# Attention and a two-layer network: tiles projected in another order, key sums behind the denominator, another order of DMAs

## The chip, the cores and the metric

The kernel runs on one core of a Trainium2 chip. The time is that of the device, in microseconds (us), as the median of several executions. An execution that is profiled beside those gives the trace; all rows below are of such an execution. Engines: PE is TensorE's matmul and PEld its weight load, DVE is VectorE, ACT is ScalarE, POOL is GpSimd, SP is SyncE, which here issues nearly all DMAs in the order of one queue.

## What is computed

Two parts follow each other. The first is linear attention over 8 batches of 8 heads with 576 rows of 64 elements: queries and keys are projected to 128 features, the largest absolute value of a row is taken off, and both exp(x) and exp(-x) are features. The second is a two-layer network over the 4608 rows of the result, with a function in between that is close to a cube for small values.

```python
def phi(x):
    proj = np.einsum('bhsd,df->bhsf', x, w_phi)
    proj = proj - np.max(np.abs(proj), axis=-1, keepdims=True)
    return np.concatenate([np.exp(proj), np.exp(-proj)], axis=-1)
q_p, k_p = (phi(q), phi(k))
kv = np.einsum('bhsf,bhsd->bhfd', k_p, v)
z = np.sum(k_p, axis=2)
num = np.einsum('bhsf,bhfd->bhsd', q_p, kv)
den = np.einsum('bhsf,bhf->bhs', q_p, z)[..., None] + 1e-06
x = (num / den)        # heads side by side: 4608 x 512
h = x @ w_in           # 512 x 2048
out = (h - np.tanh(h)) @ w_out
```

Weights of the second part come as 64-bit floats and are taken apart into 32-bit ones with integer operations on the core.

## The kernel before

**Units and periods.** The attention runs over 32 units (`units`, NU = 32), each a batch with a pair of heads. `period(i)`, for i from 0 to 32, does a step of several units at once: `a` is unit i (projection), `c` is unit i-1 (its key-value product and the transposes of its queries), `p` is unit i-2 (numerator, key sums, denominator), `r` is unit i-3 (reciprocal of the denominator), `r2` is unit i-4 (division and store of the result to `xs`). Each engine does its instructions in the order in which `period` writes them (`tc.manual_schedule`). No scheduler moves them.

**Projection.** A unit's queries and keys lie behind each other in `qk`, 1152 columns, which are 9 tiles of 128 (j = 0 to 8). Tiles 0 to 3 are queries, the first half of tile 4 is the last 64 query rows, its second half the first 64 key rows, and tiles 5 to 8 are keys. `project(u, r)` does a round r of them (`ROUNDS`, L202) into the PSUM tile `pp`, of which there is one (`ps_pj`, one buffer); DVE takes the maximum (`m`, L224), `less_max` subtracts it into `t` (L231) and so frees `pp` for the next round. A period has rounds 0, 1 and 2 with 2, 3 and 4 tiles: 8, 12 and 16 PE instructions in the trace, since each 32-bit product is two.

**Keys.** `k_exp` (ACT, L260) makes the key features `kp`: half of tile 4 from round 1, in the unit's own period; tiles 5 to 8 from round 2, one period later. `kv` (PE, L266, tile `pc`) multiplies them with `v`; `kv_copy` brings the product out. POOL adds the five key tiles: `kadd` does three additions in the period of `c`, into the tile `t` of round 2, `kadd_last` the fourth a period later. `ksum` (PE, L285, tile `pk`) adds over the partitions with four products with ones, between `kv` and round 2. `turn` transposes `kvt` and `kst` (tiles `ptk`), and `denom` (PE, L333, tile `pd`) needs its copy `kv..s` (ACT, L311).

**Queries.** `q_side` transposes them on PE (`ptr` L247, `ptt` L241) and makes `qe` on ACT (L251, L255). `num` (L318, tile `po`) uses them in the next period.

**The denominator.** `denom_copy` (ACT, L348, `dd`), a DMA that spreads it over partitions (`dn`, L353), the reciprocal on DVE (`rn`, L361), a DMA to DRAM (`rr`, L362), two DMAs that read it back as broadcasts (`rb`, L369), the product on DVE (`den_mul`, L374) and the store (`x_store`, L377).

**Weights.** One of 32 pieces of 512 KB is loaded in each period (`dec_load`, tile `raw`), and taken apart by `dec_0` (ACT, L168), `dec_1` (DVE, L172 and L173) and `dec_2`, `dec_3` (DVE, L176, L180). `split_w` then makes a high and a low part. `behind(x)` is a POOL copy of one column (`mark`, L187) which keeps POOL's later instructions behind whatever writes x.

**SP's order in a period:** dn, qk of the next unit, the store, rr, both rb, the weight piece, v of the next unit. Each waits in this queue for what it needs: rb for rr's landing, the store for `den_mul`.

The second phase (from L515) runs 12 groups of 384 rows over 16 slices of the hidden layer, and reads `xs` and the split weights.

Of the kernel before, what the change touches and what calls it, by code (L numbers as in the profile page):

```python
# [32 lines left out]
def tile_linear_attention_moe(  # L33
# [88 lines left out]
    with ExitStack() as c1:  # L122
# [79 lines left out]
        ROUNDS = ((0, 2), (2, 5), (5, 9))  # L202

        def project(u, r, where=None):
            j0, j1 = ROUNDS[r]
# [5 lines left out]
            for j in range(j0, j1):  # L211
                for e in range(2):
                    hs = slice(e * D, (e + 1) * D)
                    nc.tensor.matmul(  # L214
                        heads[e][:, (j - j0) * F : (j - j0 + 1) * F], u.qk[hs, j * P : (j + 1) * P], wph[hs, :], start=True, stop=True
                    )
# [40 lines left out]
        def k_exp(u, r):  # L257
            rows, x, j0, j1 = (slice(SR, P), u.t[1][SR:P, :, 2:3, :], 0, 1) if r == 1 else (slice(0, P), u.t[2], 1, 5)
            for s in range(2):
                nc.scalar.activation(u.kp[rows, :, j0:j1, s, :], x, AF.Exp, scale=1.0 - 2.0 * s)  # L260
# [9 lines left out]
        def kadd(u):  # L270
            x = u.t[2].rearrange("p e a f -> p (e a f)")[:, 0 : 4 * F].rearrange("p (e s f) -> p e s f", e=2, s=2)
            nc.gpsimd.tensor_tensor(x, u.kp[:, :, 1], u.kp[:, :, 2], ALU.add)
            nc.gpsimd.tensor_tensor(x, x, u.kp[:, :, 3], ALU.add)
            nc.gpsimd.tensor_tensor(x, x, u.kp[:, :, 4], ALU.add)
            u.ss = [x]

        def kadd_last(u):
            nc.gpsimd.tensor_tensor(u.ss[0], u.ss[0], u.kp[:, :, 0], ALU.add)

        def ksum(u):  # L280
            u.pk = ps_d.tile([P, 512], F32, tag="po", name=f"pk{u.i}")
            parts = u.ss or [u.kp[:, :, j] for j in range(5)]
            for a, x in enumerate(parts):
                for n in range(4):
                    nc.tensor.matmul(  # L285
                        u.pk[n * 32 : (n + 1) * 32, 0:F], ones, x[:, n // 2, n % 2, :], start=(a == 0), stop=(a == len(parts) - 1)
                    )
# [124 lines left out]
        def period(i):  # L412
# [26 lines left out]
            if 0 <= n < 4 * AHEAD:
                if n % 2 == 0:  # L440
                    lows.extend(split_w(n // 2))
                lows.pop(0)()
# [12 lines left out]
            if a:  # L455
                less_max(a, 1)
            if r:
                den_recip(r)
                den_spread(r)
            if w:  # L460
                dec_2(w)
                dec_3(w)
                if i < NU:
                    dec.append(dec_load(i))
                behind(w.d[w.f])
            if c:
                if not last:
# [205 lines left out]
```

## Time and profile before

| what | us |
|---|---|
| median of 3 runs (1160.58 to 1161.43) | 1161.35 |
| the profiled execution, its own time | 1161.82 |
| its span | 1160.00 |
| start to the first regular period (period 2) | 20.83 |
| periods 2 to 30 (20.83 to 320.80) | 299.97 |
| periods 31 and 32 (320.80 to 345.0) | 24.2 |
| second phase (from 345.0) | 815.0 |

A row of the timeline gives the start in us from the span's start, the duration, engine, line, operation, the tile written and the tiles read, and the shape; "x8" are eight instructions merged; in brackets stands how long the engine was idle before, and what ended that. A row of groups gives busy us and the mean ns of one behind the bar. A row of windows gives the stretch, its length, the busy time and instructions of PE, PEld, DVE, ACT and POOL, the granted TensorE clock, the share of the DMA engines' time and GB/s. A row of waits gives the sum, the times and the longest. A row of DMA issues ends with the median us from issue to landing.

### The profile page before, as it was taken

What the parts mean: (1) busy time and instruction counts of PE and PEld (TensorE: products, weight loads), DVE (VectorE), ACT (ScalarE), POOL (GpSimd) and SP (SyncE); (2) the same over time, 40 slices, a digit from 0 to 9 for tenths busy, and PEclk for the clock granted to TensorE, in tenths of its full rate; (3) what the DMA queues carried; (4) which work ended last, traced back from release to release, by engine and by line L of the source; (5) the groups of instructions that cost most, each with busy time, mean ns of one, the idle gap of its engine ahead of it and who ended that gap; (6) DMA issues with size and microseconds to landing.
All of it is one profiled execution on the core that took longest, in us unless ns stands there. A gap on an engine that the chain in (4) does not pass through costs nothing.

```text
span 1160.0 us, 20769 instructions
## 1 busy us (share of the span) xinstructions
PE 1139.1 (98%) x7610; PEld 947.5 (82%) x7610; DVE 862.9 (74%) x1429; ACT 818.2 (71%) x1780; POOL 428.0 (37%) x437
## 2 busy tenths in 40 slices
PE   8999999999999999999999999999999999999997
PEld 6666666666658889999999999999999999999996
DVE  6888888888868777776777777677777767777665
ACT  4777777787778767776766766676777667676664
POOL 2666666666537632222222222222222222222222
PEclk9999999999999999999999999999999999999999
DMA  4565666665742010000100010010100001000000
GB/s 155 186 197 177 207 205 211 193 197 195 224 130 66 14 35 14 34 21 8 41 15 34 14 35 21 8 42 14 35 21 35 14 8 41 14 29 1 28 1 28
DMA packets 51175, 85.60 MB, mean 74 GB/s; under 512 B 13312, under 2 KB 28032, under 8 KB 51072
## 3 DMA queue, kind: packets, MB, share of 16 engines
q1 hardware_dynamic: 50912, 84.20, 22.7%
q8 instruction: 60, 0.98, 0.4%
q14 instruction: 43, 0.35, 0.1%
q10 hardware_dynamic: 160, 0.07, 0.0%
HBM read 65.08 MB, written 19.02 MB: 72 GB/s over the span
## 4 chain that ended last, share of the span: by engine, by line
PE 84%; DMA 8%; ACT 3%; DVE 2%; SPq 1%; issue 1%; POOL 1%; DVEq 0%; POOLq 0%; ACTq 0%
PE ph L535 34%; PE po L573 11%; PE po L571 11%; PE po L570 11%; PE pp L214 4%; PE pc L266 4%; PE po L318 3%; DMA dn<-dd 3%; DMA rr<-rn 3%; PE pd L333 2%; DMA rb<-rr 2%; PE ptt L241 2%; PE pk L285 1%; SPq L369 1%; DMA qk<-in_qkT 1%
## 5 line engine op out<-in xcount | busy, mean ns | idle before, releaser
L564 POOL TENSOR_TENSOR gl<-s,gh 128x384 fp32r<-128x384 f32 x192 | 196.3, 1022 | 568.0 <-ACT gh L563 566.5
L542 ACT ACTIVATE y<-ph 128x384 f32<-128x384 f32 x192 | 94.5, 492 | 237.8 <-PE ph L535 237.6
L535 PE MATMUL ph<-xh,wli 128*128 128x384 f32 x768 | 259.1, 337 | 0.8 <-POOL wli L97 0.8
L535 PE MATMUL ph<-xh,whi 128*128 128x384 f32 x768 | 258.6, 337 | 0.0
L535 PE MATMUL ph<-xl,whi 128*128 128x384 f32 x768 | 257.9, 336 | 0.0
L551 DVE SCALAR_TENSOR_TENSOR s<-s,y 128x384 f32<-128x384 f32 x192 | 110.1, 573 | 180.6 <-ACT s L544 180.4
L570 PE MATMUL po<-who,gh 128*128 128x512 f32 x576 | 227.1, 394 | 1.7 <-ACT gh L563 1.7
L571 PE MATMUL po<-wlo,gh 128*128 128x512 f32 x576 | 226.8, 394 | 0.0
L573 PE MATMUL po<-who,gl 128*128 128x512 f32 x576 | 164.4, 393 | 0.9 <-POOL gl L564 0.9
L535 PEld LDWEIGHTS ph<-xh,whi 128*128 128x128 f32 x768 | 144.3, 188 | 8.9 <-issue 0.5
L535 PEld LDWEIGHTS ph<-xl,whi 128*128 128x128 f32 x768 | 144.2, 188 | 8.3
L535 PEld LDWEIGHTS ph<-xh,wli 128*128 128x128 f32 x768 | 144.1, 188 | 1.2 <-POOL wli L97 1.2
L260 ACT ACTIVATE kp<-t 128x1024 f32<-128x1024 f32 (+1 forms) x128 | 88.5, 751 | 79.8 <-DVE t L231 73.2
L557 DVE COPY_PREDICATED s<-mk,th 128x384 f32<-128x384 uint32 x176 | 123.8, 703 | 18.5 <-DVE th L556 0.5
L573 PEld LDWEIGHTS po<-who,gl 128*128 128x128 f32 x576 | 107.9, 188 | 27.3 <-POOL gl L564 2.5
L570 PEld LDWEIGHTS po<-who,gh 128*128 128x128 f32 x576 | 107.9, 187 | 20.6 <-ACT gh L563 3.6
L224 DVE TENSOR_REDUCE m<-pp 128x4 f32<-128x512 f32 (+3 forms) x98 | 92.0, 940 | 42.5 <-PE pp L214 41.1
L571 PEld LDWEIGHTS po<-wlo,gh 128*128 128x128 f32 x576 | 108.2, 188 | 16.3
L544 ACT ACTIVATE s<-y,bias_t 128x384 f32<-128x384 f32 x192 | 118.3, 616 | 3.0 <-POOL gl L564 3.0
L550 ACT ACTIVATE mk<-y,bias_t 128x384 f32<-128x384 f32 x192 | 117.7, 613 | 0.5 <-DVE s L557 0.5
L553 DVE SCALAR_TENSOR_TENSOR s<-s,s 128x384 f32<-128x384 f32 x176 | 99.1, 563 | 18.0 <-ACT mk L550 0.9
L554 DVE SCALAR_TENSOR_TENSOR s<-s,ph 128x384 f32<-128x384 f32 x192 | 106.2, 553 | 6.3
(356 smaller groups left out, 1733.0 us busy)
## 6 DMA issues: line engine op xcount, KB each, us to landing
qk<-in_qkT SPq DMA_DIRECT2D x31, 576.0 KB, 6.3
v<-in_v SPq DMA_DIRECT2D x32, 320.0 KB, 5.0
rb<-rr SPq DMA_DIRECT2D x64, 144.0 KB, 3.3
xs<-rb SPq DMA_DIRECT2D x32, 288.0 KB, 5.0
x<-xs SPq DMA_DIRECT2D x48, 192.0 KB, 2.4
out<-o SPq DMA_DIRECT2D x36, 256.0 KB, 2.0
rawi<-in_moe_w_in SPq DMA_DIRECT2D x16, 512.0 KB, 4.6
rawo<-in_moe_w_out SPq DMA_DIRECT2D x16, 512.0 KB, 4.8
```

The lines of the kernel that those rows point to most:

```text
L535: nc.tensor.matmul(h, wt[:, c * P : (c + 1) * P], x[:, c, 0:N], start=(i == 0), stop=(i == 3 * NCT - 1))
L542: nc.scalar.activation(y, h, AF.Square)
L544: nc.scalar.activation(s1, y, AF.Square, bias=bias_t[:, 0:1])
L550: nc.scalar.activation(mk, y, AF.Relu, bias=bias_t[:, 2:3])
L551: nc.vector.scalar_tensor_tensor(s1, s1, PC1, y, ALU.add, ALU.mult)
L553: nc.vector.scalar_tensor_tensor(gs, s2, PC2, s1, ALU.add, ALU.mult)
L554: nc.vector.scalar_tensor_tensor(gs, gs, PA, h, ALU.mult, ALU.mult)
L557: nc.vector.copy_predicated(gs, mk.bitcast(U32), hh)
L564: pin(nc.gpsimd.tensor_tensor(gl, gs, f32(gh), ALU.subtract))
L570: nc.tensor.matmul(po[t], a, wo[f][0], start=(f == 0), stop=False)
L571: nc.tensor.matmul(po[t], a, wo[f][1], start=False, stop=False)
L573: nc.tensor.matmul(po[t], gl[:, t * P : (t + 1) * P], wo[f][0], start=False, stop=(f == NF - 1))
```

## The change

Three things change.

1. The rounds take other tiles: round 0 tiles 4 and 5, round 1 tiles 0, 6 and 7, round 2 tiles 1, 2, 3 and 8. So four of the five key tiles (half of 4, and 5, 6, 7) get their features in the unit's own period, and three of the four additions are done there, into a tile of their own, `ss`; the last key tile (8) follows in the next period.
2. `ksum` moves from the period of `p`, between `kv` and round 2, to the end of the period of `c`, behind `denom`, and writes into the PSUM pool of `pc`; its copy comes early in the next period. POOL's last addition stands behind a mark on `rb` instead of one on `dec_a`.
3. SP's order in a period becomes: dn, the weight piece, v of the unit itself, the store, rr, both rb, qk of the unit after next.

`d` has three buffers instead of four. In the last period the last weight piece's `dec_0` moves behind `num_copy`.

```diff
-        ROUNDS = ((0, 2), (2, 5), (5, 9))
+        ROUNDS = ((4, 5), (0, 6, 7), (1, 2, 3, 8))
...
         def k_exp(u, r):
-            rows, x, j0, j1 = (slice(SR, P), u.t[1][SR:P, :, 2:3, :], 0, 1) if r == 1 else (slice(0, P), u.t[2], 1, 5)
-            for s in range(2):
-                nc.scalar.activation(u.kp[rows, :, j0:j1, s, :], x, AF.Exp, scale=1.0 - 2.0 * s)
+            t = u.t[r]
+            if r == 0:
+                parts = ((slice(SR, P), 0, t[SR:P, :, 0, :]), (slice(0, P), 1, t[:, :, 1, :]))
+            elif r == 1:
+                parts = ((slice(0, P), slice(2, 4), t[:, :, 1:3, :]),)
+            else:
+                parts = ((slice(0, P), 4, t[:, :, 3, :]),)
+            for rows, j, x in parts:
+                for s in range(2):
+                    o = u.kp[rows, :, j, s, :]
+                    nc.scalar.activation(o, x, AF.Exp, scale=1.0 - 2.0 * s)
...
-        def kadd(u):
-            x = u.t[2].rearrange("p e a f -> p (e a f)")[:, 0 : 4 * F].rearrange("p (e s f) -> p e s f", e=2, s=2)
-            nc.gpsimd.tensor_tensor(x, u.kp[:, :, 1], u.kp[:, :, 2], ALU.add)
-            nc.gpsimd.tensor_tensor(x, x, u.kp[:, :, 3], ALU.add)
-            nc.gpsimd.tensor_tensor(x, x, u.kp[:, :, 4], ALU.add)
-            u.ss = [x]
-
-        def kadd_last(u):
-            nc.gpsimd.tensor_tensor(u.ss[0], u.ss[0], u.kp[:, :, 0], ALU.add)
-
-        def ksum(u):
-            u.pk = ps_d.tile([P, 512], F32, tag="po", name=f"pk{u.i}")
-            parts = u.ss or [u.kp[:, :, j] for j in range(5)]
-            for a, x in enumerate(parts):
-                for n in range(4):
-                    nc.tensor.matmul(
-                        u.pk[n * 32 : (n + 1) * 32, 0:F], ones, x[:, n // 2, n % 2, :], start=(a == 0), stop=(a == len(parts) - 1)
-                    )
+        def kadd(u, js):
+            if u.ss is None:
+                u.ss = p2.tile([P, 2, 2, F], F32, tag="ss", name=f"ss{u.i}")
+                nc.gpsimd.tensor_tensor(u.ss, u.kp[:, :, 0], u.kp[:, :, 1], ALU.add)
+            for j in js:
+                nc.gpsimd.tensor_tensor(u.ss, u.ss, u.kp[:, :, j], ALU.add)
+
+        def ksum(u, pool=ps_c, tag="pc"):
+            u.pk = pool.tile([P, 512], F32, tag=tag, name=f"pk{u.i}")
+            for n in range(4):
+                nc.tensor.matmul(u.pk[n * 32 : (n + 1) * 32, 0:F], ones, u.ss[:, n // 2, n % 2, :], start=True, stop=True)
...
-            if 1 <= i < NU - 1:
-                load(units[i + 1])
+            if 3 <= i <= NU:
+                dec.append(dec_load(i - 1))
+            if 1 <= i < NU:
+                load_v(a)
+            if p:
+                ksum_copy(p)
...
-            if p:
-                if w:
-                    behind(w.a)
-                kadd_last(p)
...
             if c:
                 k_exp(c, 2)
+                if w:
+                    behind(r2.rb if r2 else w.a)
+                kadd(c, (4,))
...
                 less_max(a, 1)
+                k_exp(a, 0)
...
-                if i < NU:
-                    dec.append(dec_load(i))
                 behind(w.d[w.f])
             if c:
-                if not last:
-                    kadd(c)
                 kv(c)
-            if p:
-                ksum(p)
-            if i + 1 < NU:
-                load_v(units[i + 1])
+                kv_copy(c)
+            if last:
+                ksum(c, ps_d, "po")
+                ksum_copy(c)
             if a:
                 k_exp(a, 1)
-            if c:
-                kv_copy(c)
-            if p:
-                ksum_copy(p)
-            if 2 <= i < NU + 1:
+                kadd(a, (2, 3))
+            if 2 <= i < NU:
                 dec_0(dec[i - 1])
             if a:
                 project(a, 2, (ps_d, "po") if i == 0 else None)
                 less_max(a, 2)
-            if last:
-                ksum(c)
-                ksum_copy(c)
+            if i + 2 < NU:
+                load(units[i + 2])
...
             if p:
                 denom(p)
+            if c and not last:
+                ksum(c)
```

PE's order in period 20, from round 1 on; a name holds the unit's number (`pp20_1` is round 1 of unit 20, `pk18` the key sums of unit 18). Before:

```order
L214 MATMUL pp20_1_2852<-wph_118,qk20_2687 128x128 x6
L266 MATMUL pc19_2879<-kp1_130,v19_2616 64x256 x10
L285 MATMUL pk18_2890<-t18_2_2637,ones_111 32x128 x4
L214 MATMUL pp20_2_2905<-wph_118,qk20_2687 128x128 x8
L303 MATMUL ptk18s_2918<-ident_60,kst18_2901 128x128
L308 MATMUL ptk18s_2918<-ident_60,kvt19_2899 128x128 x2
L247 MATMUL ptr19_2925<-ident_60,t19_1_2723 128x128 x2
L241 MATMUL ptt19_0_2928<-ident_60,t19_0_2681 128x128 x2
...
L333 MATMUL pd18_2944<-qe18_2786,kv18s_2919 32x288 x8
L214 MATMUL pp21_0_2953<-wph_118,qk21_2828 128x128 x4
```

And now, in the same place:

```order
L214 MATMUL pp20_1_2963<-wph_118,qk20_2734 128x128 x6
L274 MATMUL pc19_2989<-kp1_130,v19_2791 64x256 x10
L214 MATMUL pp20_2_3010<-wph_118,qk20_2734 128x128 x8
L304 MATMUL ptk18s_3025<-ident_60,kst18_2939 128x128
L309 MATMUL ptk18s_3025<-ident_60,kvt19_3000 128x128 x2
L247 MATMUL ptr19_3032<-ident_60,t19_0_2783 128x128 x2
...
L334 MATMUL pd18_3051<-qe18_2888,kv18s_3026 32x288 x8
L288 MATMUL pk19_3060<-ss19_2861,ones_111 32x128 x4
L214 MATMUL pp21_0_3065<-wph_118,qk21_2880 128x128 x4
```

`pk` went from between `pc` and round 2 to between `pd` and the next round 0, and it is now that of the unit of `pc`. The number of products is the same.

SP's order, from a reciprocal's load of period 19 to that of period 20. Before:

```order
L353 DMA dn16_2685<-dd16_2683 128x1x9
L196 DMA qk20_2687<-in_qkT 128x1152
L377 DMA xs1_76<-rb15_2588 128x576
L362 DMA rr16_2725<-rn16_2726 128x9
L369 DMA rb16_2729<-rr16_2725 64x576 x2
L161 DMA rawo9_2735<-in_moe_w_out 128x512
L200 DMA v20_2757<-in_v5 128x640
L353 DMA dn17_2826<-dd17_2824 128x1x9
```

And now:

```order
L354 DMA dn16_2787<-dd16_2785 128x1x9
L156 DMA rawi9_2789<-in_moe_w_in 128x4x128
L200 DMA v19_2791<-in_v5 128x640
L378 DMA xs1_76<-rb15_2693 128x576
L363 DMA rr16_2835<-rn16_2836 128x9
L370 DMA rb16_2839<-rr16_2835 64x576 x2
L196 DMA qk21_2880<-in_qkT 128x1152
L354 DMA dn17_2933<-dd17_2931 128x1x9
```

qk and the pair of weight piece and v changed places around dn, the store, rr and rb. The weight piece `rawo9`, which stood in period 19 for a `dec_0` in period 20, is now loaded in period 20 itself, and qk a period earlier.

ACT's order in period 20, from the denominator's copy to `turn`'s. Before:

```order
L348 ACTIVATE dd17_2824<-pd17_2806 128x288
L260 ACTIVATE kp1_130<-t19_2_2778 128x2x4x128 x2
L344 COPY d18_2849<-po18_0_2839 128x288
L344 COPY d18_2849<-po18_1_2840 128x288
L260 ACTIVATE kp0_129<-t20_1_2861 64x2x128 x2
L291 COPY kvt19_2899<-pc19_2879 128x256
L295 COPY kst18_2901<-pk18_2890 128x128
L168 ACTIVATE dec_ao9_2903<-rawo9_2735 128x512
L311 COPY kv18s_2919<-ptk18s_2918 128x384
```

And now:

```order
L349 ACTIVATE dd17_2931<-pd17_2908 128x288
L296 COPY kst18_2939<-pk18_2917 128x128
L268 ACTIVATE kp1_130<-t19_2_2878 128x2x128 x2
L345 COPY d18_2960<-po18_0_2950 128x288
L345 COPY d18_2960<-po18_1_2951 128x288
L268 ACTIVATE kp0_129<-t20_0_2929 64x2x128 x2
L268 ACTIVATE kp0_129<-t20_0_2929 128x2x128 x2
L292 COPY kvt19_3000<-pc19_2989 128x256
L268 ACTIVATE kp0_129<-t20_1_2972 128x2x2x128 x2
L168 ACTIVATE dec_ao9_3008<-rawo9_2935 128x512
L312 COPY kv18s_3026<-ptk18s_3025 128x384
```

Four long or narrow key exps became eight shorter ones, four of them between the numerator's copies and `kv_copy`; the copy of the key sums went to the front.

More of the change, by code (lines that the diff above doesn't have):

```diff
@@ L200, in load_v @@
             nc.sync.dma_start(u.v.rearrange("p j e d -> p (j e d)"), v5[u.i])
-        ROUNDS = ((0, 2), (2, 5), (5, 9))
+        ROUNDS = ((4, 5), (0, 6, 7), (1, 2, 3, 8))
         def project(u, r, where=None):
-            j0, j1 = ROUNDS[r]
+            js = ROUNDS[r]
             if where is None:
@@ L210, in project @@
                 heads = [where[0].tile([P, 512], F32, tag=where[1], name=f"pp{u.i}_{r}_{e}") for e in range(2)]
-            for j in range(j0, j1):
+            for o, j in enumerate(js):
                 for e in range(2):
@@ L214, in project @@
                     nc.tensor.matmul(
-                        heads[e][:, (j - j0) * F : (j - j0 + 1) * F], u.qk[hs, j * P : (j + 1) * P], wph[hs, :], start=True, stop=True
+                        heads[e][:, o * F : (o + 1) * F], u.qk[hs, j * P : (j + 1) * P], wph[hs, :], start=True, stop=True
                     )
-            n = j1 - j0
+            n = len(js)
             m = p2.tile([P, 2, n], F32, tag=f"m{r}", name=f"m{u.i}_{r}")
@@ L227, in less_max @@
         def less_max(u, r):
-            n = ROUNDS[r][1] - ROUNDS[r][0]
+            n = len(ROUNDS[r])
             t = p2.tile([P, 2, n, F], F32, tag=f"t{r}", name=f"t{u.i}_{r}", bufs=2)
@@ L234, in q_tile @@
         def q_tile(u, e, j):
-            r = 0 if j < 2 else 1
-            return u.t[r][:, e, j - ROUNDS[r][0], :]
+            r = next(r for r, js in enumerate(ROUNDS) if j in js)
+            return u.t[r][:, e, ROUNDS[r].index(j), :]
         def qt(u, e):
@@ L341, in num_copy @@
         def num_copy(u):
-            u.d = tail.tile([P, S], F32, tag="d", name=f"d{u.i}", bufs=4)
+            u.d = tail.tile([P, S], F32, tag="d", name=f"d{u.i}", bufs=3)
             for c in range(2):
@@ L433, in period @@
                 x_store(r2)
-            if p:
-                if w:
-                    behind(w.a)
-                kadd_last(p)
             n = i - 3
[L439 to L442, printed above, removed]
+            if 0 <= n < 4 * AHEAD and n % 2 == 0:
+                lows.extend(split_w(n // 2))
             if c:
                 k_exp(c, 2)
+                if w:
+                    behind(r2.rb if r2 else w.a)
+                kadd(c, (4,))
+            if 0 <= n < 4 * AHEAD:
+                lows.pop(0)()
             if p:
@@ L454, in period @@
                 project(a, 1, (ps_tr, "tr") if i == 0 else None)
-            if a:
                 less_max(a, 1)
+                k_exp(a, 0)
             if r:
@@ L495, in period @@
                 num_copy(c)
+                dec_0(dec[i - 1])
                 denom_copy(p)
```

## The prediction

> **What bounds the kernel now.** I read the page first, then busy time by stage, then one undisturbed period in order of time, then a disturbed one.
>
> ```profile
> PE 1139.1 (98%) x7610; PEld 947.5 (82%) x7610; DVE 862.9 (74%) x1429; ACT 818.2 (71%) x1780; POOL 428.0 (37%) x437
> ```
>
> PE is busy almost always, so I look for what little it waits, by stage:
>
> ```profile
> 20.83:320.80 299.97, 293.43 (x3162) 193.01 (x3162) 249.50 (x345) 228.81 (x510) 188.35 (x201) 1.00 0.61 194
> ...
> 345.00:1160.00 815.00, 806.35 (x4036) 727.39 (x4032) 584.17 (x1039) 564.65 (x1218) 225.71 (x213) 1.00 0.08 24
> ```
>
> The second row is the second phase (DMA 8% busy), which the change does not touch. The first is the 29 periods 2 to 30, with the DMA engines 61% busy; periods 31 and 32 lie between. One clean period of PE and DVE:
>
> ```profile
> 196.29 0.71 PE L214 MATMUL pp<-wph,qk 64*128 64x128 f32 x8
> 199.18 0.75 DVE L374 TENSOR_TENSOR rb<-d,rb 128x576 f32<-128x576 f32 x1
> 199.90 2.38 PE L266 MATMUL pc<-kp,v 128*64 128x256 f32 x20
> 201.01 0.96 DVE L231 TENSOR_TENSOR t<-pp,m 128x768 f32<-128x768 f32 x1
> 202.21 0.43 PE L285 MATMUL pk<-t,ones 128*32 128x128 f32 x8
> 202.56 1.16 PE L214 MATMUL pp<-wph,qk 64*128 64x128 f32 x16
> 203.77 1.23 DVE L224 TENSOR_REDUCE m<-pp 128x8 f32<-128x1024 f32 x1 [0.41 <-PE pp L214]
> 204.04 0.38 PE L247 MATMUL ptr<-ident,t 128*128 128x128 f32 x2
> 204.25 1.04 PE L241 MATMUL ptt<-ident,t 128*128 128x128 f32 x8
> 205.10 1.23 DVE L231 TENSOR_TENSOR t<-pp,m 128x1024 f32<-128x1024 f32 x1
> 205.22 1.18 PE L333 MATMUL pd<-qe,kv17s 128*32 128x288 f32 x16
> 206.43 0.71 PE L214 MATMUL pp<-wph,qk 64*128 64x128 f32 x8
> ```
>
> From round 0 to the next round 0 it is 10.14 us (196.29 to 206.43). PE looks full, yet the period closes through DVE: round 2's subtraction ends at 206.33 (205.10 + 1.23), and round 0 of the next unit, which needs its PSUM tile, starts 0.10 later, 1.21 after pd. Where DVE was done in good time, pd to pp takes 1.11:
>
> ```profile
> 143.62 1.18 PE L333 MATMUL pd<-qe,kv11s 128*32 128x288 f32 x16
> 144.73 0.38 PE L214 MATMUL pp<-wph,qk 64*128 64x128 f32 x2
> ```
>
> So each clean period holds 0.10 us of PE waiting for DVE. Beside that, 299.97 - 29 x 10.14 = **5.9 us** are lost in disturbed periods. One of them:
>
> ```profile
> 102.97 0.53 SPq L161 DMA_DIRECT2D rawo<-in_moe_w_out  x1
> 104.07 0.59 SPq L353 DMA_DIRECT2D dn<-dd  x1
> 105.41 1.73 DVE L374 TENSOR_TENSOR rb<-d,rb 128x576 f32<-128x576 f32 x1 [0.36 <-DMA rb<-rr]
> 105.25 1.27 POOL L278 TENSOR_TENSOR t<-t,kp 128x512 f32<-128x512 f32 x1
> ...
> DVE rn L361 <- DMA dn<-dd: 5.5, 9, 1.4
> DVE rb L374 <- DMA rb<-rr: 2.8, 4, 1.4
> ```
>
> The small dn transfer stands on the SP queue behind a weight load (512 KB) and v (320 KB). The reciprocal waited for it 9 times, 5.5 us in all; rr and rb are then late too, and den_mul, beginning late, meets a key addition on POOL and takes 1.73 instead of 0.75.
>
> **The change, part by part.** *PE.* The four key-sum products (8 instructions) cost 202.56 - 202.21 = 0.35 between pc and round 2. They move behind pd. Round 2 then follows pc directly, 0.35 earlier; pc's own 2.31 (199.90 to 202.21) stays. From pd to the next round 0 the time becomes 1.11 + 0.35 = 1.46 if PE pays the usual price of a new tile shape between pd and pk, and 0.10 less if not. From ptr to ptt, of one shape, two transposes take 204.25 - 204.04 = 0.21; eight at that pace are 0.84 to 0.88, but pd starts 0.97 behind the first of them (204.25 to 205.22): some 0.10 for going over to another shape. Both pd and pk are 128*32, so I take 1.36. The Trainium skill, TensorEngine Tiling (Array Packing), section Key Properties, says that a change of the tiling mode drains TensorE and another tile of the same mode does not; by that rule the value is 1.36, without it 1.46, and no row here has pd and pk side by side. The period changes by -0.35 + (1.36 - 1.21) = **-0.20** (with 1.46: -0.10), to 9.94. Over 29 periods: **-5.8 us**, at least -2.9.
>
> Will DVE allow it? Round 2's maximum now waits 0.41 for PE, so it can follow by 0.35; round 2 to the next round 0 needs 3.87 by DVE (202.56 to 206.43), and PE gets there after 4.02. DVE keeps 0.15 + 0.06 of slack per period. Round 2 itself needs round 1's subtraction, ended 201.97; PE comes at 202.21, against 202.56 before. So the cover that swallowed a late den_mul (0.41 to 0.5 us) shrinks to 0.2: what is late next is rb.
>
> *DMA order.* dn now has only qk (576 KB) between it and rb instead of 832 KB and one issue less ahead of it on SP, and qk is asked for a period earlier. POOL's key addition now stands behind a mark on rb, so it can't meet den_mul. Both causes of the row of 1.73 go. The bytes of a period are the same. I take the loss in the 29 periods from 5.9 to 2.5, **-3.4 us**; ends: all gone (-5.9), and, since the slack is down from 0.4 to 0.2 in 29 periods, 3 us worse.
>
> The weight load moves the other way: from the end of the period before to just behind dn, about where qk stands now.
>
> ```profile
> 198.01 0.42 SPq L196 DMA_DIRECT2D qk<-in_qkT  x1
> 202.80 0.37 ACT L291 COPY kvt<-pc 128x256 f32<-128x256 f32 x1
> 203.37 0.68 ACT L168 ACTIVATE dec_ai<-rawi 128x512 f32<-128x512 f32 x1
> 204.24 0.48 ACT L311 COPY kv17s<-ptk17s 128x384 f32<-128x384 f32 x1 [0.19 <-PE ptk17s L308]
> 204.89 1.09 ACT L251 ACTIVATE qe<-ptt 128x512 f32<-128x512 f32 x2
> ...
> qk<-in_qkT SPq DMA_DIRECT2D x28, 576.0 KB, 7.9
> rawo<-in_moe_w_out SPq DMA_DIRECT2D x14, 512.0 KB, 4.8
> ```
>
> Issued 1.7 after the period's start (198.01 - 196.29) it lands at 6.5 by its own median of 4.8. ACT reaches dec_0 behind kv_copy (pc ends at 202.28, 6.0 in; the copy is 0.37) and two exps of 512 columns (0.98 to the start of the next, by the pair of L251): 7.25 in. Slack 0.75. Cost: nothing, but some 2 us of cover are gone (the issue now stands behind dn, not ahead of v: 102.97 to 104.07 and dn's own 0.59).
>
> *ACT.* Key exps of a period: a pair of 1024 and a pair of 256 become three pairs of 256 and a pair of 512.
>
> ```profile
> 202.06 0.72 ACT L260 ACTIVATE kp<-t 64x256 f32<-64x256 f32 x2 [1.77 <-DVE t L231]
> 197.64 2.05 ACT L260 ACTIVATE kp<-t 128x1024 f32<-128x1024 f32 x2
> ```
>
> 3 x 0.72 + 1.09 = 3.25 instead of 2.77. The four new early ones fill the 1.77 in which ACT waited for round 1. dec_0 and kv_copy before `turn` end at 7.8, the turn's copy at 8.3; pd, now 8.58 in (205.22 - 0.35 - 196.29), waits for it with 0.3 to spare. Cost nothing. POOL keeps four additions; its one behind den_mul ends at about 5.0 in, pk comes at 9.6. *d* with three buffers: den_mul of unit n-3 is done a period before. Nothing.
>
> *The end.*
>
> ```profile
> 328.36 1.16 PE L214 MATMUL pp<-wph,qk 64*128 64x128 f32 x16 [1.23 <-DVE rn L361]
> 335.36 1.95 PE L266 MATMUL pc<-kp,v 128*64 128x256 f32 x16 [0.44 <-ACT kp L260]
> 337.48 1.27 PE L285 MATMUL pk<-kp,ones 128*32 128x128 f32 x40
> ```
>
> Period 31 lost 1.23 to the same chain: **-1.3** (0 to -1.5). In the last period kv no longer waits for exps of 1024 columns (about 0.5 with the gap before), and the last unit's 20 key products become 4, of 1.27 some 1.0 less: **-1.5** (0 to -2.2); dec_0 of the last weight goes behind num_copy, where ACT is idle.
>
> *The start.* Round 0 is now tiles 4 and 5, so the first products need all three pieces of qk.
>
> ```profile
> 0.74 1.33 SPq L196 DMA_DIRECT2D qk<-in_qkT  x3
> 4.58 0.71 PE L214 MATMUL pp<-wph,qk 64*128 64x128 f32 x8
> 12.15 0.69 DVE L231 TENSOR_TENSOR t<-pp,m 128x512 f32<-128x512 f32 x1
> 13.86 0.94 PE L214 MATMUL pp<-wph,qk 64*128 64x128 f32 x12
> DMA to landing us min/median/max: 2.7/3.3/4.8
> ```
>
> The third piece, issued by 2.07 at the latest, lands around 5 instead of PE's 4.58. DVE then ends unit 1's round 0 at 13.3 instead of 12.84, still ahead of 13.86: 0 (at worst +0.5).
>
> Sum: -5.8 - 3.4 - 1.3 - 1.5 = -12.0. The profiled execution took 1161.82 by its own time (span 1160.00), 0.47 over the median of the runs, 1161.35. 1161.82 - 12.0 = **1149.8**, and from the median it would be 1149.3.
>
> **Rivals.** *A, the waits stay:* rb lands late as often as now and the thinner slack lets it through; the PE term holds, the loss is 5.9 to 8.9 us, the last period gives 1.5. For it: the same bytes stand ahead of rr. Against: rn's waits for dn alone are 5.5. 1161.8 - 5.8 - 1.5 (+ 0 to 3) = 1154.5 to 1157.5.
>
> *B, slower: the weight load is late on ACT.* dec_0 stands before the turn's copy, on which pd waits. It decides once the load lands later than 7.55 in (7.25 and 0.3), a lag of 5.85 against 4.8. qk's own lag, with much traffic around it, is 7.9; a load that took halfway, 6.35, would land at 8.05, put pd 0.5 late and make the period 10.44: 29 x 0.3 = +8.7, less 2.8 at the end and the dn gain: about 1166. For it: 576 KB of qk now stand right ahead. Against: rb and v stand around it today, and its lag is still 4.8. The Trainium skill, DMA: Bandwidth & Descriptors, section Rules for kernel authors, advises issuing a DMA early and waiting late; this change does the reverse for the weights, and no run here shows that yet.
>
> *C, nothing:* pk behind pd pays the switch (-2.9), new waits for rb (+3) eat that, and the last periods give 0 to 2: 1159.8 to 1161.9.
>
> **Chances.** Forecast, with its own range 1145 to 1154: 0.6. A 0.18, B 0.12, C 0.10. A measurement of this kernel can tell about 0.2% (2.3 us) from no change: the forecast and A are faster (0.78), C is within it (0.10), B slower (0.12). The range of 8 in 10 takes the forecast and A with the near edge of C: 1144.5 to 1159.
>
> **What will show it.** pc to round 2 in 2.31; pd to pk 1.01 (right) or 1.11; clean periods of 9.94; rn's waits for dn nearly gone; den_mul never at 1.7. Wrong would be: ACT idle before dec_0 waiting for raw, pd waiting for ACT, or DVE waiting for rb in many periods.

## The result, and the profile after

The changed kernel takes 1170.88 us (median of 5 runs, 1165.36 to 1172.38), the kernel before 1161.09 (1160.18 to 1161.43). The ratio is 1.0077, with an interval of 1.0053 to 1.0102: **slower**, where I had forecast 1149.8 and at most 1159.0. The profiled execution took 1172.38 (span 1170.6), so it lies 1.5 us over the median.

By stage, from the windows view of after (stretch, length, then busy time of PE, PEld, DVE, ACT and POOL, clock, DMA share, GB/s):

```profile
23.10:334.07 310.97, 290.46 (x3162) 196.33 (x3162) 247.91 (x345) 241.56 (x624) 174.63 (x203) 0.99 0.60 188
```

The 29 periods took 310.97 us instead of 299.97, while PE was busy for 3 us less. What stands ahead of them took 2.27 more (23.10 against 20.83), what stands behind them 836.5 instead of 839.2. So 2.3 + 11.0 - 2.7 = 10.6, the difference of the spans: the loss is in the periods. Of the 2.7, 2.4 lie in periods 31 and 32 (21.7 instead of 24.2, up to the first product of the second phase).

A clean period of after, PE's rows of the timeline:

```profile
226.70 0.71 PE L214 MATMUL pp<-wph,qk 64*128 64x128 f32 x8
...
230.31 2.38 PE L274 MATMUL pc<-kp,v 128*64 128x256 f32 x20
232.62 1.16 PE L214 MATMUL pp<-wph,qk 64*128 64x128 f32 x16
...
235.28 1.18 PE L334 MATMUL pd<-qe,kv19s 128*32 128x288 f32 x16
236.27 0.40 PE L288 MATMUL pk<-ss,ones 128*32 128x128 f32 x8
236.60 0.71 PE L214 MATMUL pp<-wph,qk 64*128 64x128 f32 x8
```

It is 9.90 long (226.70 to 236.60), where 9.94 was forecast: pc to round 2 takes 2.31, pd to pk 0.99, pd to the next round 0 1.32. But only 10 of the 29 periods are like this to 0.05; before, 19 were clean at 10.13. 310.97 - 29 x 9.90 = 23.9 us are lost in the others, against 6.1 before (with 10.133, the clean period to one digit more; the 5.9 of the prediction was with 10.14). What they wait for, in the waits view of after over the same stretch:

```profile
DVE rb L375 <- DMA rb<-rr: 18.1, 17, 2.2
...
PE pp L214 <- DVE rn L362: 12.8, 12, 2.0
...
ACT dec_ao L168 <- DMA rawo<-in_moe_w_out: 7.4, 7, 2.7
...
ACT dec_ai L168 <- DMA rawi<-in_moe_w_in: 2.7, 3, 1.7
...
PE pd L334 <- ACT kv8s L312: 2.1, 1, 2.1
```

DVE waits for rb 17 times instead of 4, and ACT waits for the weights 10 times instead of never; PE's wait for ACT is spread over nine tiles, 6.7 us in all, of which the longest is shown. The waits for dn (5.5 us before) are down to one. One such period, rows of DVE, ACT, PE and SP:

```profile
199.27 0.33 SPq L363 DMA_DIRECT2D rr<-rn  x1
...
201.38 0.68 ACT L168 ACTIVATE dec_ao<-rawo 128x512 f32<-128x512 f32 x1 [0.43 <-DMA rawo<-in_moe_w_out]
...
201.97 0.46 ACT L312 COPY kv16s<-ptk16s 128x384 f32<-128x384 f32 x1
...
202.48 1.18 PE L334 MATMUL pd<-qe,kv16s 128*32 128x288 f32 x16 [0.40 <-ACT kv16s L312]
...
203.92 1.11 SPq L370 DMA_DIRECT2D rb<-rr  x2
...
205.13 0.53 SPq L196 DMA_DIRECT2D qk<-in_qkT  x1
...
205.76 0.58 SPq L354 DMA_DIRECT2D dn<-dd  x1
...
206.44 0.42 SPq L156 DMA_DIRECT2D rawi<-in_moe_w_in  x1
...
207.95 0.76 DVE L375 TENSOR_TENSOR rb<-d,rb 128x576 f32<-128x576 f32 x1 [1.17 <-DMA rb<-rr]
...
210.71 1.16 PE L214 MATMUL pp<-wph,qk 64*128 64x128 f32 x16 [0.92 <-DVE rn L362]
...
212.32 0.69 ACT L168 ACTIVATE dec_ai<-rawi 128x512 f32<-128x512 f32 x1 [0.50 <-DMA rawi<-in_moe_w_in]
```

rr is issued at 199.27 and rb, which waits in SP's queue for rr's landing, at 203.92, 4.65 later (the median of the 29 periods is 3.36, before 2.80). So den_mul waits 1.17, round 1's subtraction is late, and PE idles 0.92 before round 2. And the weight piece of 206.44 is not there until 212.32, 5.88 behind its issue: rival B's threshold was 5.85.

The longest wait cost more than itself. PE waited 2.11 us for a copy of ACT (`kv8s`), and about 1 us behind its end the granted TensorE clock fell to 0.50 for 3.4 us (the last row is one of the windows view):

```profile
118.13 1.18 PE L334 MATMUL pd<-qe,kv8s 128*32 128x288 f32 x16 [2.11 <-ACT kv8s L312]
...
120.79 3.05 PE L319 MATMUL po<-qe,kv8s 128*64 128x288 f32 x16
...
119.20:122.60 3.40, 3.40 (x28) 1.99 (x22) 1.66 (x3) 2.76 (x9) 0.00 (x0) 0.50 0.63 113
```

po took 3.05 instead of 2.16, and the period that began at 119.63 lasted 11.30 although PE waited for nothing in it: 1.4 of the 23.9 us.

### The profile page after: what moved, and what is told of

The parts are those of the page before. It is cut to its first block, busy times and chain, and to the rows that moved or that the text cites. A ratio compares the mean times of both kernels' runs of the same rounds, so it can differ in the third digit from the quotient of the medians.

```text
span 1170.6 us, 21022 instructions
## 1 busy us (share of the span) xinstructions
PE 1137.5 (97%) x7578; PEld 951.9 (81%) x7578; DVE 863.3 (74%) x1429; ACT 833.4 (71%) x1908; POOL 417.3 (36%) x441
## 4 chain that ended last, share of the span: by engine, by line
PE 78%; DMA 11%; DVE 5%; ACT 2%; issue 2%; POOL 1%; SPq 1%; DVEq 0%; ACTq 0%; POOLq 0%
PE ph L534 33%; PE po L572 11%; PE po L570 11%; PE po L569 11%; DMA rb<-rr 5%; DMA rr<-rn 3%; PE pp L214 3%; PE po L319 2%; DVE m L224 2%; DMA rawo<-in_moe_w_out 2%; PE pd L334 2%; PE pc L274 1%; PE ptt L241 1%; DVE t L231 1%; DVE rb L375 1%
## 5 line engine op out<-in xcount | busy, mean ns | idle before, releaser
L283 POOL TENSOR_TENSOR ss<-ss,kp 128x512 f32<-128x512 f32 x96 | 122.7, 1278 | 9.4 <-ACT kp L268 4.4
L268 ACT ACTIVATE kp<-t 128x256 f32<-128x256 f32 (+2 forms) x256 | 108.4, 481 | 17.6 <-DVE t L231 16.4
L214 PEld LDWEIGHTS pp<-wph,qk 64*128 64x128 f32 x1152 | 74.0, 190 | 49.6 <-issue 19.0
```

What stands on the lines that cost most here:

```text
L214: nc.tensor.matmul(heads[e][:, o * F : (o + 1) * F], u.qk[hs, j * P : (j + 1) * P], wph[hs, :], start=True, stop=True)
L283: nc.gpsimd.tensor_tensor(u.ss, u.ss, u.kp[:, :, j], ALU.add)
```

## The experiments

All were compared with the kernel before on the same chip. "Lost" is the length of periods 2 to 30 less 29 clean ones, in the profiled execution; the waits are sums and times in the same periods. Different rows come from different chips, on which the kernel before took 1160.04 to 1162.10, so rows are compared by their ratios. Each loss is that of one execution.

| kernel | time, us | ratio to before, interval | clean period | lost | DVE for rb | DVE for dn | ACT for weights |
|---|---|---|---|---|---|---|---|
| before | | | 10.13 | 6.1 | 2.8, 4 | 5.5, 9 | 0 |
| after | 1170.88 | 1.0077, 1.0053 to 1.0102 | 9.90 | 23.9 | 18.1, 17 | 0.3, 1 | 10.1, 10 |
| e1_old_dmas | 1161.55 | 0.9991, 0.9972 to 1.0010 | 9.90 | 14.6 | 13.3, 16 | 6.1, 12 | 0 |
| e2_new_dmas_alone | 1168.09 | 1.0056, 1.0036 to 1.0075 | 10.13 | 14.5 | 9.9, 15 | 0.6, 2 | 10.4, 11 |
| e3_first_tiles | 1169.25 | 1.0050, 1.0028 to 1.0073 | 9.90 | 20.0 | 14.1, 15 | 0 | 10.0, 13 |
| e4_weights_behind_rb | 1159.90 | 0.9979, 0.9957 to 1.0001 | 9.90 | 12.2 | 3.7, 5 | 10.7, 15 | 0 |
| e5_pe_slowed | 1162.15 | 1.0016, 0.9997 to 1.0035 | 10.11 | 6.9 | 6.8, 6 | 4.7, 10 | 0 |
| e6_den_mul_later | 1159.91 | 0.9997, 0.9979 to 1.0015 | 9.90 | 15.0 | 0 | 10.7, 13 | 11.5, 12 |
| e7_dn_own_queue | 1160.48 | 1.0008, 0.9988 to 1.0027 | 9.90 | 13.1 | 0.4, 1 | 15.8, 18 | 0 |
| e8_rn_behind_dec_2 | 1157.51 | 0.9967, 0.9952 to 0.9983 | 9.90 | 9.6 | 5.9, 9 | 5.2, 11 | 0 |
| e9_three_windows | 1179.24 | 1.0144, 1.0114 to 1.0173 | 9.90 | 34.7 | 0 | 29.6, 22 | 1.8, 2 |
| e10_weights_early_wait | 1162.53 | 1.0007, 0.9988 to 1.0026 | 9.90 | 17.8 | 0 | 3.3, 4 | 15.1, 17 |
| e11_period_of_lead | 1147.20 | 0.9884, 0.9863 to 0.9904 | 9.90 | 0.0 | 0 | 0 | 0 |
| e12_lead_alone | 1155.43 | 0.9951, 0.9938 to 0.9965 | 10.13 | 0.0 | 0 | 0 | 0 |

My theory after the result was that SP's new order had put the small rr behind more bulk (the weights and v) and the weights too close to their use ("order"). The rival: the shorter period leaves DVE less room, so that lags which were there before now reach PE ("slack").

**e1_old_dmas.** The compute of after with SP's order of before.

```diff
-            if 3 <= i <= NU:
-                dec.append(dec_load(i - 1))
-            if 1 <= i < NU:
-                load_v(a)
+            if 1 <= i < NU - 1:
+                load(units[i + 1])
...
                 dec_3(w)
+                if i < NU:
+                    dec.append(dec_load(i))
...
+            if i + 1 < NU:
+                load_v(units[i + 1])
...
-            if i + 2 < NU:
-                load(units[i + 2])
```

> The changed kernel with SP's order of before (dn, qk of the next unit, the store, rr, both rb, the weight piece, v of the next unit); tiles, additions and key sums as changed. Theory 'order': v and the weight piece now stand between dn and rr, rr lies behind their packets (rr to rb 3.35 us median instead of 2.78) and the weights reach ACT late; with the old order the clean period stays 9.90 and the loss in periods 2 to 30 falls from 23.9 to under 7 us: 1147 to 1156 us. Theory 'slack': the shorter period leaves DVE 0.2 us of slack instead of 0.4, so that any order loses as much: 1164 to 1172 us, loss over 17.

It came out between the two. The waits for the weights went, but 14.6 us were still lost, with rb late 16 times:

```profile
DVE rb L375 <- DMA rb<-rr: 13.3, 16, 1.5
...
DVE rn L362 <- DMA dn<-dd: 6.1, 12, 1.0
```

**e2_new_dmas_alone** is the other half: before, with the same lines the other way round.

> The kernel before with the new order of DMAs alone (dn, weight piece, v of the unit, the store, rr, rb, qk of the unit after next). Theory 'order': clean periods of 10.13 and a loss of 12 us or more in periods 2 to 30, rr to rb over 3.1 median: 1166 to 1178 us. Theory 'slack': the old slack swallows it, loss 5 to 8: 1159 to 1163 us.

Here too neither theory's figures came: the loss went from 6.1 to 14.5. From the waits view of e2:

```profile
DVE rb L374 <- DMA rb<-rr: 9.9, 15, 1.4
...
PE pp L214 <- DVE rn L361: 9.6, 13, 0.8
...
ACT dec_ai L168 <- DMA rawi<-in_moe_w_in: 7.0, 7, 1.6
...
ACT dec_ao L168 <- DMA rawo<-in_moe_w_out: 3.4, 4, 1.1
```

So the order by itself costs 8.4 us, the compute by itself costs 8.5 us of new stalls, and both together 17.8. Each theory names about half of the loss, and in these executions they nearly add (1.4 of the 17.8 are the half clock shown above).

**e3_first_tiles.** After, with unit 0's qk loaded in the order in which its rounds use it (tiles 4 and 5, then 6 to 8, then 0 to 3).

```diff
-            cut = (0, PC) if u.i else (0, 2 * P, 5 * P, PC)
-            for o, w in zip(cut, cut[1:]):
+            cut = ((0, PC),) if u.i else ((4 * P, 6 * P), (6 * P, PC), (0, 4 * P))
+            for o, w in cut:
```

> The changed kernel with unit 0's qk loaded in the order of its new rounds (tiles 4 and 5, then 6 to 8, then 0 to 3). Theory 'start': period 2 began 2.27 us later because the first products wait for the third piece and DVE runs behind from there; with tiles 4 and 5 first, period 2 starts at 20.8 to 21.5 instead of 23.1, and the time falls by 1.5 to 2.3 us (0.1 to 0.2%). Rival: the first DMAs came late in that one execution by chance, period 2 starts at 22.5 to 23.5 whatever the pieces.

Period 2 began at 21.36 instead of 23.10. That is no proof: the nine other kernels of this study that kept after's three pieces began it between 20.25 (e9) and 22.81 (e5). The +2.3 at the start of after can't be put down to the pieces (the last section says what goes with a late start). In the periods nothing changed, with 20.0 lost, and the time stayed slower than before.

**e4_weights_behind_rb.** After, with the weight piece alone back behind rb, ahead of qk.

```diff
-            if 3 <= i <= NU:
-                dec.append(dec_load(i - 1))
...
+            if 2 <= i < NU:
+                dec.append(dec_load(i))
             if i + 2 < NU:
                 load(units[i + 2])
```

> The changed kernel with only the weight piece back behind rb (ahead of qk); v stays behind dn, qk stays a unit ahead. Theory 'order': rr has 512 KB less ahead of it, and ACT never waits for the weights (9 waits, 9.1 us before); but dn lies behind 1088 KB. Loss in periods 2 to 30 between 6 and 14 us: 1152 to 1162 us. If the late weights on ACT were nearly all of it: loss about 15 (1162); if rr's queue was: loss under 10. Theory 'slack': no change of the loss beyond ACT's 9 us: 1161 to 1168 us.

The loss halves, and the time falls by some 11 us (by the ratios). ACT's waits are gone and rr comes back in 2.34. But now dn is late, since the weights and qk (1088 KB) are issued ahead of it:

```profile
DVE rn L362 <- DMA dn<-dd: 10.7, 15, 2.0
...
DVE rb L375 <- DMA rb<-rr: 3.7, 5, 1.4
```

**e5_pe_slowed.** e1 with the first three products of pk issued twice, so that a period is as long as before.

```diff
-            for n in range(4):
+            for n in (0, 1, 2, 0, 1, 2, 3):
```

> The compute of after with SP's order of before (as in e1_old_dmas), and in each period the first three of the four products of pk are issued twice, 0.26 us more of PE. In e1 a clean period was 9.90, den_mul found its rb late 16 times (13.3 us in all) and the 29 periods lost 14.6 us; before, with 10.13, it was 4 times and 6.1 us. Theory 'slack': the shorter period leaves DVE 0.23 us less between a reciprocal and the den_mul that needs its rb, and what DVE is late goes to PE at once. Then with clean periods of 10.14 to 10.17 the loss goes back to 5 to 9 us with rb late at most 7 times, and the time stays within 2 us of e1's, 1160 to 1164, though PE does 7.5 us more. Rival 'compute': something else in the new compute makes rb late (its exps, its additions, the place of rr); then the loss stays at 13 or more and the time is 1166 to 1170.

The windows of e1 and of e5 over their 29 periods:

```profile
21.13:322.79 301.66, 288.93 (x3162) 195.84 (x3162) 247.16 (x345) 242.40 (x625) 174.44 (x202) 1.00 0.61 193
...
22.81:322.94 300.13, 293.99 (x3336) 201.60 (x3336) 247.05 (x345) 240.40 (x625) 174.38 (x202) 1.00 0.61 194
```

PE does 5.1 us more than in e1 (293.99 against 288.93), and the periods take 300.13 against 301.66. A clean period is 10.11, the loss 6.9, nearly that of before. So e1's extra stalls come with the shorter period and not with anything else in the new compute: PE saves 6.8 us (29 x 0.233), and 14.6 - 6.9 = 7.7 came back as waits. This rests on one execution of each; the ratios of the runs (0.9991 and 1.0016, each to 0.0019) are too coarse to decide it.

**e6_den_mul_later.** After, with den_mul moved behind the reciprocal and dec_2 in its old place, so that rb has 2.9 us longer.

```diff
                 dec_1(w)
-            if r2:
-                den_mul(r2)
-                x_store(r2)
+                dec_2(w)
...
-                    behind(r2.rb if r2 else w.a)
+                    behind(w.a)
...
                 den_spread(r)
-            if w:
-                dec_2(w)
+            if r2:
+                den_mul(r2)
+                x_store(r2)
+            if w:
                 dec_3(w)
```

> After, but den_mul stands behind the reciprocal instead of behind dec_1, some 2.9 us later in the period, and dec_2 takes its old place; the store of xs goes behind rb with it. rb thus has 2.9 us longer to come. In after, den_mul waited 18.1 us for rb in 17 periods, dec_0 10.1 us for its weights in 10, pd 6.7 us for ACT, and the 29 periods lost 23.9. Theory 'both, one beside the other': the waits for rb go (under 3 us), those of dec_0 stay (8 to 12 us), the loss comes down to 9 to 14 and the time by 10 to 15, to 1155 to 1161. Rival 'weights': the late weights alone set the loss and rb is late because ACT and PE are; then the loss stays above 18 and the time above 1165. Rival 'rb alone': dec_0's waits vanish with rb's; loss under 6, time 1150 to 1154.

POOL's mark, which stood on rb, stands on `dec_a` here. rb is never late, and ACT's waits stay (11.5 us): the two do stand beside each other. But the loss fell only to 15.0, as dn became late: the store of xs had gone behind rb, and with qk it stood ahead of dn.

**e7_dn_own_queue.** e4 with dn issued by ACT, on a queue on which nothing else stands.

```diff
-            nc.sync.dma_start(dn, u.dd.rearrange("(n r) c -> n r c", r=32)[:, 0, :])
+            nc.scalar.dma_start(dn, u.dd.rearrange("(n r) c -> n r c", r=32)[:, 0, :])
```

> e4_weights_behind_rb (after, with the weight piece behind rb and ahead of qk), with the load of dn issued by ACT on its own queue right behind the copy that it reads, instead of by SP. In e4, with 1088 KB issued on SP's queue between rb and dn, dn took a median of 4.2 us from issue to its last packet, and the reciprocal waited for it in 15 periods, 10.7 us, of 12.2 us lost. Theory 'queue': a small transfer waits for the bulk issued ahead of it on the same queue; on another queue dn takes under 3 us, the waits of rn fall below 3 us, the loss to 3 to 6 and the time by 6 to 9, to 1151 to 1154. Rival 'engines': it waits because the 16 DMA engines are busy, whatever the queue; dn still takes over 3.7 us, the time stays at 1157 to 1162. Rival 'ACT pays': dn is quick, but issuing it holds up ACT's exps by more than ACT has to spare, clean periods become 10.0 or longer, time 1158 or more.

The queue is not it. dn took a median of 5.1 us from issue to its last packet, not less than e4's 4.2, and its first packet came 4.0 us behind the issue. A period of e7, with dn behind bulk issued on the other queue just ahead:

```profile
124.40 0.52 SPq L161 DMA_DIRECT2D rawo<-in_moe_w_out  x1
...
125.01 0.38 SPq L196 DMA_DIRECT2D qk<-in_qkT  x1
...
125.26 0.54 ACTq L354 DMA_DIRECT2D dn<-dd  x1
...
131.45 0.22 DVE L362 RECIPROCAL rn<-dn 128x9 f32<-128x9 f32 x1 [1.12 <-DMA dn<-dd]
```

**e8_rn_behind_dec_2.** e4 with the reciprocal one DVE operation later.

```diff
-            if r:
-                den_recip(r)
-                den_spread(r)
             if w:
                 dec_2(w)
+            if r:
+                den_recip(r)
+                den_spread(r)
+            if w:
                 dec_3(w)
```

> e4_weights_behind_rb, with the reciprocal (and rr and rb with it) one DVE operation later, behind dec_2 (0.64 us). In e4 dn came too late for the reciprocal in 15 periods (10.7 us), while rb had a median of 1.0 us to spare (landed 5.76 us behind the reciprocal, used 6.79 behind it) and was late 5 times (3.7 us). Theory 'two windows': the time from dn's issue to den_mul is shared between two waits, and 0.64 moved from one to the other serves both; rn's waits fall below 5 us, rb's stay below 6, the loss in the 29 periods is 4 to 9 instead of 12.2 and the time 1153 to 1157. Rival 'only moved': every late dn is later by as much for rb; what rn no longer waits, den_mul waits, the loss is 11 or more, and the time within 2 us of e4's 1159.9.

Half right: dn's waits fell from 10.7 to 5.2, rb's rose from 3.7 to 5.9, and 9.6 is lost, just over the 9 that I allowed. It beats the kernel before by 0.33%.

**e9_three_windows.** e4 with the reciprocal behind dec_3 and den_mul behind the reciprocal, so that each transfer has more time than it took in any run. POOL's mark on rb moves behind den_mul with it.

```diff
                 dec_1(w)
-            if r2:
-                den_mul(r2)
-                x_store(r2)
+                dec_2(w)
...
-                    behind(r2.rb if r2 else w.a)
+                    behind(w.a)
...
-            if r:
-                den_recip(r)
-                den_spread(r)
             if w:
-                dec_2(w)
                 dec_3(w)
-                behind(w.d[w.f])
+            if r:
+                den_recip(r)
+                den_spread(r)
+            if r2:
+                den_mul(r2)
+                x_store(r2)
+            if w:
+                behind(r2.rb if r2 else w.d[w.f])
```

> After with the weight piece behind rb (as in e4), and DVE's order in a period dec_1, dec_2, round 1, dec_3, reciprocal, den_mul, round 2: the reciprocal stands 0.7 us later than in e4, den_mul 3.9 us later, so that dn, rb and the weights each have more time than they took in any run (dn's last packet came up to 4.9 us behind its issue, which is at 1.0 of the period, and the reciprocal stands at 6.3; rb landed up to 8.4 behind the reciprocal, and den_mul now stands a whole period behind it). Theory 'three waits': the stalls of the 29 periods were these three waits and nothing else; clean periods stay at 9.90, the loss falls to 1 to 5 us, the time to 1148 to 1153. Rival 'they come back': the new place of the store and of den_mul makes something else late (round 2's maximum, the store's bulk ahead of dn), the loss stays at 8 or more, the time at 1155 or more.

My theory failed and the kernel is the slowest of all. One turn of its wheel:

```profile
122.61 0.21 DVE L362 RECIPROCAL rn<-dn 128x9 f32<-128x9 f32 x1 [1.28 <-DMA dn<-dd]
...
122.85 0.33 SPq L363 DMA_DIRECT2D rr<-rn  x1
...
124.40 1.10 SPq L370 DMA_DIRECT2D rb<-rr  x2
...
125.55 0.58 SPq L378 DMA_DIRECT2D xs<-rb  x1
...
126.18 0.43 SPq L161 DMA_DIRECT2D rawo<-in_moe_w_out  x1
...
126.71 0.40 SPq L196 DMA_DIRECT2D qk<-in_qkT  x1
...
127.20 0.60 SPq L354 DMA_DIRECT2D dn<-dd  x1
...
134.23 0.22 DVE L362 RECIPROCAL rn<-dn 128x9 f32<-128x9 f32 x1 [1.76 <-DMA dn<-dd]
```

The reciprocal waits for dn, SP's rr for the reciprocal, rb for rr, and behind rb stand three bulk transfers (1376 KB) and then the next dn, which takes 7.03 to the next reciprocal. The circle closes in 11.62 us (122.61 to 134.23) and is longer than a period of PE: it sets the pace by itself. I had given each wait more time, but moved all the bulk to where dn stands behind it.

**e10_weights_early_wait.** e9 with the weight piece behind dn again, as in after (e4's edit undone).

> e9_three_windows with one edit: the weight piece stands behind dn again, ahead of v, as in after. Theory 'weights late on ACT': dec_0 waits 8 to 13 us in all for its piece, pd for ACT's copy behind it, the 29 periods lose 7 to 13 us more than in e9, and the time is 6 to 12 above e9's. Rival 'room': with the other two waits gone, ACT takes a late piece without holding up pd; the loss is within 3 us of e9's, and so is the time.

It is faster than e9, so the expected difference of times did not come; e9 was the wrong thing to stand on. By itself it shows the weights' price: rb is never late and dn 4 times, and ACT waits 15.1 us in 17 periods for its piece, pd 14.3 us for ACT behind it, of 17.8 lost. The rival "room" falls.

```profile
ACT dec_ai L168 <- DMA rawi<-in_moe_w_in: 10.2, 9, 2.5
...
ACT dec_ao L168 <- DMA rawo<-in_moe_w_out: 4.9, 8, 1.0
```

**e11_period_of_lead.** The compute of after, SP's order of before, and the reciprocal a period later, ahead of round 0; rb and den_mul follow a period later too.

```diff
+            if r2:
+                den_recip(r2)
             if a:
                 a.kp = kpb[i % 2]
...
-            if r2:
-                den_mul(r2)
-                x_store(r2)
+            if r2:
+                den_spread(r2)
+            if r3:
+                den_mul(r3)
+                x_store(r3)
...
-            if r:
-                den_recip(r)
-                den_spread(r)
```

> The compute of after and SP's order of before, with a period more between dn and its reciprocal, and another between rb and den_mul: the reciprocal stands at the start of the next period, ahead of round 0's maximum, so SP issues rr, dn, qk of the next unit, rb, the store, the weights and v, and nothing on SP waits for a transfer issued in the last 2 us but rb for rr (d has four buffers, dd and kst one). In e9 the wait for dn closed a circle through SP's queue: dn late, so rr late, so rb and the bulk behind it late, so the next dn late, in periods of up to 11.6 us. Theory 'lead': with the circle cut, what PE does sets the period; clean periods of 9.90 nearly throughout, waits for dn, rb and the weights under 2 us in all, the loss in the 29 periods under 4, the time 1145 to 1151. Rival 'bandwidth': the 2 MB of a period don't fit into 9.9 us beside each other whatever waits for what; the waits show up at qk, v or the weights, the loss stays at 8 or more, the time at 1154 or more.

Its 29 periods in the windows view:

```profile
21.28:308.40 287.12, 287.12 (x3162) 194.99 (x3162) 249.46 (x344) 238.17 (x624) 175.11 (x202) 1.00 0.67 202
```

PE is busy for 287.12 of 287.12 us; all 29 periods are clean. SP's rows and the reciprocal of one period show how much earlier the transfers are asked for:

```profile
200.66 0.59 SPq L357 DMA_DIRECT2D dn<-dd  x1
...
209.00 0.20 DVE L365 RECIPROCAL rn<-dn 128x9 f32<-128x9 f32 x1
...
209.24 0.33 SPq L366 DMA_DIRECT2D rr<-rn  x1
...
211.82 0.47 SPq L373 DMA_DIRECT2D rb<-rr  x1
```

dn has 8.3 us to come. rr to rb is no quicker than before the change, with a median of 2.80. dn itself is quicker: its last packet is there 1.7 us behind the issue (median), against 3.9 in e1. The new place of the reciprocal also moved SP's issues apart; the load of v is issued 3.5 us ahead of this dn (197.13 to 200.66), where in a period of e1 it was 0.5 (209.12 to 209.58). The rival "bandwidth" falls too: 202 GB/s instead of 194 go through. **e12_lead_alone** is the kernel before with the same lines moved.

> Before, with the same period of lead for the denominator and nothing of the change. Theory 'lead': clean periods of 10.13, a loss under 3 in place of 6.1, period 31 without its wait, the time 4 to 7 below before's: 1154 to 1157, and 6 to 10 above e11's, which is what the change's compute brings where nothing waits for a transfer (0.23 x 29 = 6.8, and 2.7 at the end). Rival 'not the chain': the loss stays at 5 or more, the time at 1159 or more.

```profile
20.60:314.46 293.86, 293.10 (x3161) 192.90 (x3162) 246.92 (x344) 228.12 (x508) 187.16 (x202) 1.00 0.65 198
```

Clean periods of 10.13, nothing lost, 1155.43 us. Between e12 and e11, on one chip, lie 8.2 us: that is what the change's compute brings where no transfer is waited for. e11 beats both kernels, by 1.2% the one before.

## Why the prediction was wrong

**PE's term was right.** -0.20 per period was forecast, -0.233 measured (10.13 to 9.90). pk stands 0.99 behind pd, where I had forecast 1.01 without a price for the tile shape and 1.11 with it. The Trainium skill, TensorEngine Tiling (Array Packing), section Key Properties, says that another tile of the same mode doesn't drain TensorE; the trace agrees, with this 0.99. den_mul never met POOL either: its longest takes 0.76.

**The end was right in sum:** -1.3 and -1.5 forecast, -2.4 measured in periods 31 and 32, though period 31 still waited 0.92 for DVE. There is luck in that: with the same compute at the end, these two periods took 20.7 (e4) to 25.3 us (e5), against 21.7 in after.

**The step that failed** is the DMA term, "I take the loss in the 29 periods from 5.9 to 2.5, -3.4 us": it rose by 17.8. Three things were wrong in it.

1. I counted the bytes between rb and dn (832 to 576 KB) and dropped dn's waits, rightly. I did not count those between dn and rr, and rival A even says that "the same bytes stand ahead of rr"; they rose by the same 256 KB (864 to 1120 with the store). The lag of each follows the bulk issued ahead of it, in all kernels here without a stage of lead (e7, with dn on another queue, left out). The table has medians over the 29 periods, of dn from its issue to its last packet and of the issues of rr and rb; rb's own 288 KB, which stand ahead of dn in every row, are not counted:

| kernels | KB ahead of dn | dn, us | KB ahead of rr | rr to rb, us |
|---|---|---|---|---|
| after, e2, e3 | 576 | 3.3, 3.3, 3.4 | 1120 | 3.4, 3.3, 3.7 |
| before, e1, e5 | 832 | 3.8, 3.9, 3.9 | 864 | 2.8, 3.2, 2.8 |
| e6, e10 | 864 | 4.0, 4.0 | 832 | 2.8, 2.6 |
| e4, e8 | 1088 | 4.2, 4.5 | 608 | 2.3, 2.3 |
| e9 | 1376 | 5.4 | 320 | 1.5 |

The two lags sum to 6.5 to 7.1 us in every row: a period's 1696 KB stand ahead of the one or the other, and in these runs another order only moved the lag from one of the two to the other.

2. I saw that DVE's slack falls "from 0.4 to 0.2 in 29 periods" and priced it at up to 3 us. e1 and e5 show 7.7. The lags of rb scatter: before, its last packet came 6.4 us behind the reciprocal's end in the median and at 7.0 or later in 3 of 28 cases, and in a clean period DVE wants it at 7.2. In e1 DVE wants it at 6.9, and 13 of 28 came at that or later, so the edge of the slack lay in the thick of them: a period shorter by 0.23 turned 4 waits into 16. Part of that may be the lag itself, which was longer in the shorter period: the median of rb is 6.7 in e1, and rr to rb takes 3.2 there against 2.8 before and in e5. How much each does, the runs don't separate.

3. **Rival B's mechanism was real** and I gave it 0.12. It said that the weights decide once their lag passes 5.85; I took 4.8 from a place in the queue where qk did not stand ahead. In the 10 periods in which ACT waited, it began 5.6 to 7.8 us behind the issue of its piece, in eight of them later than 5.85. I priced it as if every period paid 0.3; e10, in which little else waits, lost about 14 us to it in 17 periods. The Trainium skill's advice that I had set against the change (DMA: Bandwidth & Descriptors, Rules for kernel authors: issue early, wait late) is borne out: ACT waits 15.1 us for the weights in e10 and never in e11.

Rival A (rb stays late) was right as well; it and B happened at once, and I had let only one of them happen at a time. The start was forecast at 0 and took 2.27 us more; the last section shows how far it scatters.

So the compute's gain was there: e11, with the change's compute, SP's old order and a stage of lead, takes 1147.2. That this lies close to the 1149.8 forecast is luck, since the lead took away the stalls of before too and was no part of the change. In the change the gain was lost to transfers that the shorter period and the new order made late together.

## What to carry to other kernels

Where small transfers in a chain stand among bulk, count the bytes issued ahead of each one, not only of the one that is late now; moving bulk from one to the other moves the wait. Time taken from the bound engine is slack taken from everything that waits beside it, so look up how the lags scatter before the gain is written down. Here a chain that runs around through one in-order queue was cured by a stage of lead; the other orders that I tried (e4 and e6 to e10) left 9.6 to 34.7 us lost.

## What the runs showed of the hardware

- A transfer of 4.5 KB on a queue of its own (e7, ACT's) came no sooner than on SP's queue behind 1088 KB: first packet 4.0 us behind its issue against 3.5, last 5.1 against 4.2. So the bulk on one queue seems to hold up a transfer on the other; in which part of the way, the trace doesn't show. The Trainium skill, DMA: Bandwidth & Descriptors, section Queues, rings and completion order, says that each DMA engine takes turns between the queues that have work for it. By that alone I would expect dn's first packet sooner on ACT's queue than behind the bulk on SP's; here it came no sooner.
- The time to period 2 scattered between 20.25 and 23.10 us, and it goes with PE's pace in the first 10 us. In after the warm-up's second group of eight products took 1.89 us instead of 1.05 before, and the first eight products of round 0 took 2.17 instead of 0.71. In e5, the other late start (22.81), the warm-up's eight took 1.89 too; in the nine runs in which they took 1.05, period 2 began at 20.25 to 21.41. Why PE gets to its pace later in some executions, the traces don't show. The warm-up's eight, first before, then after:

```profile
5.23 1.05 PE L140 MATMUL warm<-zt 128*128 128x256 bf16 x8
...
6.96 1.89 PE L140 MATMUL warm<-zt 128*128 128x256 bf16 x8
```

- A long wait of PE can come with a halved granted clock. In the 29 periods the clock was 0.50 for 3.4 us or more once each in after, e4, e6 and e10 and twice in e9, each time beginning at most 1.1 us before or behind the end of a wait of PE of 1.74 to 2.47 us. Not every wait of that length did it: one of 1.98 us in after (it ended at 222.72) was not followed by it.
